# A third row tile loaded plainly and transposed on the array, so that three tiles' keys share the first weight chunks of a two-branch linear-attention kernel

## The chip, the core and the metric

The kernel runs on one core of a Trainium2 chip. The metric is the device time of one execution in microseconds, the median of several runs. The engines are called as the profile calls them: PE (matrix multiply), PEld (its weight loads), DVE (vector), ACT (activation), POOL, and SP, which only issues transfers. "SPq" and "ACTq" are the transfer queues of SP and ACT.

## What is computed

Two branches A and B have the same shape and the same input `x` (2048 rows of 640, bf16). Cut to what matters:

```python
def branch(x, wqkv, wo):                        # wqkv: 640 x 1920, 32 heads of 20
    q, k, v = split(x @ wqkv)
    phi = lambda t: where(t > 0, t + 1, exp(t)) + 1e-6
    pq, pk = phi(q), phi(k)
    kv, z = pk^T v, sum over rows of pk          # per head
    o = (pq @ kv) / (pq . z + 1e-6)
    return o @ wo

g = sigmoid((x * gate_w).sum(-1))
out = g * branch(x, A_wqkv, A_wo) + (1 - g) * branch(x, B_wqkv, B_wo)
```

## The kernel before

All work is cut into row tiles of 128 rows of `x` (16 tiles, `t` = 0 to 15) and contraction chunks of 128 of the 640 columns (5 chunks, `c` = 0 to 4).

The first stage computes the keys of both branches. It needs `x` with its columns on the partitions, in the buffer `XT`, as the stationary operand, and the key columns of `wqkv` in `WKW`, as the moving operand. One key step (`k_step(X, t, c, ps)`, lines 535 and 536) multiplies chunk c of tile t by chunk c of the weights of branch X: a matmul of 512 columns and one of 128 (129 for B, whose extra column is the gate). Five steps make one tile of one branch, accumulated in a pair of PSUM banks; the whole stage is 16 x 2 x 5 = 160 steps. After a tile, `k_post` makes phi of it: an exponential on ACT (L568) and two operations on DVE (L571, L579), after which the pair of banks is free.

How `XT` comes about differs by tile. Tiles 0 and 1 come by plain loads into `XN` (`ld_x`, tile 0 on SP's queue, tile 1 on ACT's) and are transposed on PE against an identity matrix (`x_tp`, L479), five transposes for each tile, which go into three PSUM banks; three copies (L496) take them to `XT`, on DVE for tile 0 and on ACT for tile 1. Tiles 2 to 15 come by transposing transfers from memory (`xt_dma`), and one later plain load (`xr`) brings their rows into `XN`, which the next stage reads.

SP issues the loads in the order written: x tile 0, the five 160 KB chunks of A's key weights, the five of B's, the seven transposing transfers, the rest. While the loads are issued, each is tied behind the one before on its queue (`o.behind`), so this order is the program's.

PE's order is the order of the calls: a planner picks, for the other engines, whichever of their operations can start first by its own costs, but for PE always the next one written. Its start is written out by hand. Warm-up matmuls (L466) come first, then the transposes of tiles 0 and 1, then A's keys of both tiles chunk by chunk (c outside, t inside), so that each landing chunk serves two tiles; `gate_col` (a small matmul, L516, and a DVE copy, L519, which put the gate vector beside B's weights) stands after the second chunk. Then come B's keys of tiles 0 and 1, also chunk by chunk, and then `k_unit(X, t)` for the other tiles, A and B in turn, each with its five steps in one go.

The later stages (the products of keys and `x`, line 643; queries, line 797; the small weights, 705 and 740; outputs, 957) follow on PE in the order written.

Of the kernel before, what the change touches and what calls it, by code (L numbers as in the profile page):

```python
# [6 lines left out]
ACT = mybir.ActivationFunctionType  # L7
# [3 lines left out]
S = 2048  # L11
D = 640
H = 32
NT = 16
NB = 4
NC = 5
# [60 lines left out]
class Sched:  # L77
# [7 lines left out]
    def op(self, eng, fn, cost, ins=(), outs=(), after=(), prio=None, name="", dma=None):  # L85
        if eng == "ACT" and dma is None:
            after = list(after) + self.consts
        o = Op(eng, fn, cost, list(ins), list(outs), after, len(self.ops) if prio is None else prio, name, dma)
        self.ops.append(o)
        return o  # L90
# [174 lines left out]
def body(nc, A_x, A_wqkv, A_wo, B_x, B_wqkv, B_wo, gate_w, out, log=None):  # L265
    no_start_barrier(nc)
    x = A_x[0]
# [8 lines left out]
    XN = sb("XN", [128, NT, XS_W], bf)  # L276
# [66 lines left out]
    def psw(b, w):  # L343
        return PS[:, b.slot : b.slot + b.n, :].rearrange("p a b -> p (a b)")[:, 0:w]
# [3 lines left out]
    def dma(q, name, dst, src, nbytes, ins=(), outs=(), after=(), issue=450.0, transpose=False, prio=None):  # L348
        timing = (330.0, 1500.0) if not transpose else (140.0, 1500.0) if loading else (1000.0, 1150.0)

        def fn(e):
            d = dst() if callable(dst) else dst
            with nc.allow_non_contiguous_dma(reason="layout"):
                return e.dma_start(d, src() if callable(src) else src, transpose=transpose)  # L354

        o = op(q, fn, 0.0, ins, outs, after, prio=prio, name=name, dma=(issue, nbytes) + timing)
        if loading:
            o.behind = chain.get(q)
            chain[q] = o
        return o  # L360

    def mm_cost(n):
        return n / 2.4 + 2.5

    def act_cost(n):
        return 190 + 0.833 * n

    def dve1(n):
        return 155 + 1.04 * n

    def dve4(n):
        return 150 + 0.27 * n


    bxn = [Buf("xn%d" % t) for t in range(NT)]
# [18 lines left out]
        outs=[bid],  # L394
# [9 lines left out]
    def ld_x(q, t):  # L404
        dma(q, "x%d" % t, XN[:, t, 0:D], x[128 * t : 128 * t + 128, :], 163840, outs=[bxn[t]])

    def ld_wk(q, X, c, after=()):
        dma(q, "wk%s%d" % (X, c), WK[X][:, c, 0:D], wqkv[X][128 * c : 128 * c + 128, D : 2 * D], 163840, outs=[bwk[X, c]], after=after)

    def xt_dma(t0, t1):  # L410
        dma(
            "SP",
            "xt%d" % t0,
            XT[:, :, 128 * t0 : 128 * t1],
            x[128 * t0 : 128 * t1, :],
            (t1 - t0) * 163840,
            outs=bxt[t0:t1],
            issue=(t1 - t0) * 1250.0,
            transpose=True,
        )  # L420
# [7 lines left out]
    for c in range(NC):  # L428
        if c == 0:
            ld_x("SP", c)  # L430
        ld_wk("SP", "A", c)
    for c in range(NC):
        ld_wk("SP", "B", c)
    for t0, t1 in ((2, 3), (3, 4), (4, 5), (5, 6), (6, 8), (8, 12), (12, 16)):
        xt_dma(t0, t1)
    dma("SP", "xr", XN[:, 2:NT, 0:D], x[256:S, :].rearrange("(t p) d -> p t d", p=128), 14 * 163840, outs=bxn[2:])
    for X in XS:
        dma("SP", "wq" + X, WQ[X][:, :, :], w3(X, 0), 819200, outs=[bwq[X]])
    for X in XS:
# [1 line left out]
    for X in XS:  # L441
        for r in range(2):
# [7 lines left out]
                outs=[bwo[X, r]],  # L450
# [11 lines left out]
    def warm(n, w=4):  # L462
        for i in range(n):
            op(
                "PE",
                lambda e: e.matmul(psw(bw, 128 * w), ONE[:, 0:1].to_broadcast([128, 128]), ONE[:, 0:1].to_broadcast([128, 128 * w]), start=True, stop=True),  # L466
                107.0 * w,
                ins=[bone],
                outs=[bw],
                name="warm",  # L470
            )

    def x_tp(t):
        for lo, hi in ((0, 1), (1, 3), (3, 5)):
            bt = Buf("tp", "ps")
            for c in range(lo, hi):
                op(
                    "PE",
                    lambda e, c=c, lo=lo, bt=bt: e.matmul(  # L479
                        PS[:, bt.slot, 128 * (c - lo) : 128 * (c - lo) + 128],  # L480
                        XN[:, t, 128 * c : 128 * c + 128],
                        IDN[:, :],
                        start=True,
                        stop=True,
                    ),
                    100.0,
                    ins=[bxn[t], bid],
                    outs=[bt],
                    name="tp%d" % t,
                )  # L490
            half = Buf("xth")

            def copy(e, lo=lo, hi=hi, bt=bt):
                o = XT[:, lo:hi, 128 * t : 128 * t + 128]
                i = PS[:, bt.slot, 0 : 128 * (hi - lo)].rearrange("p (c s) -> p c s", c=hi - lo)
                return e.activation(o, i, ACT.Copy) if t else e.tensor_copy(o, i)  # L496

            op(
                "ACT" if t else "DVE",
                copy,  # L500
                act_cost(128 * (hi - lo)) if t else dve1(128 * (hi - lo)),
                ins=[bt],
                outs=[half],
                name="tpc%d" % t,
            )
            bxt[t].parts = getattr(bxt[t], "parts", []) + [half] * (hi - lo)
# [22 lines left out]
    def k_step(X, t, c, ps):  # L529
        w = D + 1 if X == "B" else D  # L530

        def fn(e):
            a = psw(ps, w)
            l = XT[:, c, 128 * t : 128 * t + 128]
            e.matmul(a[:, 0:512], l, WK[X][:, c, 0:512], start=(c == 0), stop=(c == NC - 1))  # L535
            return e.matmul(a[:, 512:w], l, WK[X][:, c, 512:w], start=(c == 0), stop=(c == NC - 1))  # L536

        xin = [bxt[t].parts[c] if hasattr(bxt[t], "parts") else bxt[t]]
        op(
            "PE",  # L540
            fn,
            mm_cost(512) + mm_cost(128),
            ins=xin + [bwk[X, c]] + ([bgc] if X == "B" else []),
            outs=[ps],
            name="k%s%d_%d" % (X, t, c),
        )
# [3 lines left out]
    def k_post(X, t, ps):  # L550
        ek = Buf("ek", "ek")
        ek2 = Buf("ek2")
        pk = Buf("pk%s%d" % (X, t))
        bpk[X, t] = pk
        first = []
        if X == "B":
            b = Buf("ge")
            bge.append(b)
            op(
                "ACT",  # L560
                lambda e: e.activation(GE[:, t : t + 1], psw(ps, D + 1)[:, D : D + 1], ACT.Exp, scale=-1.0),
                200.0,
                ins=[ps],
                outs=[b],
                name="ge",
            )
            first = [b]
        op("ACT", lambda e: e.activation(EK[:, ek.slot, :], psw(ps, D), ACT.Exp), act_cost(D), ins=[ps] + first, outs=[ek], name="ke")  # L568
        op(
            "DVE",  # L570
            lambda e: e.tensor_scalar(EK[:, ek.slot, :], EK[:, ek.slot, :], 1.0, EPS, op0=ALU.min, op1=ALU.add),  # L571
            dve4(D),
            ins=[ek],
            outs=[ek2],
            name="kt",
        )
        op(
            "DVE",
            lambda e: e.scalar_tensor_tensor(PKt[X][:, t, :], psw(ps, D), 0.0, EK[:, ek.slot, :], op0=ALU.max, op1=ALU.add),  # L579
            dve1(D),  # L580
            ins=[ps, ek, ek2],
            outs=[pk],
            name="ks",
        )

    def k_unit(X, t):
        ps = Buf("k", "ps", 2)
        for c in range(NC):
            k_step(X, t, c, ps)
        k_post(X, t, ps)  # L590

    warm(4)
    warm(1, 2)
    pss = [Buf("k", "ps", 2) for _ in range(2)]
    x_tp(0)
    warm(1, 1)
    x_tp(1)
    for c in range(2):
        for t in range(2):
            k_step("A", t, c, pss[t])  # L600
    gate_col()
    for c in range(2, NC):
        for t in range(2):
            k_step("A", t, c, pss[t])
    for t in range(2):
        k_post("A", t, pss[t])
    pss = [Buf("k", "ps", 2) for _ in range(2)]
    for c in range(NC):
        for t in range(2):
            k_step("B", t, c, pss[t])  # L610
    for t in range(2):
        k_post("B", t, pss[t])
    for t in range(2, NT):
        for X in XS:
            k_unit(X, t)

# [10 lines left out]
        outs=[bgg2],  # L627
# [490 lines left out]
def bass_gated_mix__linear_attn_block__linear_attn_block__prompt_kernel(nc, *args):  # L1118
    body(nc, *args)
# [28 lines left out]
```

## Time and profile before

| | |
|---|---|
| time, median of 3 runs | 188.19 us (188.06 to 188.35) |
| span of the profiled execution | 186.3 us |
| PE busy | 183.4 us, 98% of the span |
| DVE, ACT busy | 136.9 us, 94.8 us |
| share of PE in the chain that ended last | 96% |

A busy time is the sum of an engine's instructions in the span. "The chain that ended last" is followed back from the last instruction: at each step to whatever released it. Since PE is nearly all of that chain, what changes the end is time that PE spends without an instruction, and instructions added to PE. Both lie, as far as this change is concerned, in the first microseconds, so the views that matter are PE's timeline there and the times in which the first loads land.

### The profile page before, as it was taken

How to read it: one execution, taken by the hardware profiler on the slowest of the kernel's cores; microseconds unless marked ns; L12 is line 12 of the kernel's file. 1: busy time of each engine (PE TensorE's matmuls, PEld its weight loads, DVE VectorE, ACT ScalarE, POOL GpSimd, SP SyncE). 2: the span in 40 equal slices, each digit the busy share in tenths (PEclk: the TensorE clock that was granted, in tenths of full speed). 3: DMA queues.
4: the chain of work that ended last, by engine and by line, in shares of the span. 5: the costliest groups of instructions: out<-in, count | busy, mean ns of one | idle time of the engine just before them, and what ended most of it. 6: DMA issues, size and time to landing. Idle time of an engine off the chain costs nothing.

```text
span 186.3 us, 3272 instructions
## 1 busy us (share of the span) xinstructions
PE 183.4 (98%) x1297; PEld 106.4 (57%) x1297; DVE 136.9 (73%) x264; ACT 94.8 (51%) x167; POOL 0.8 (0%) x10
## 2 busy tenths in 40 slices
PE   8999999999999999999999999999999999999995
PEld 4555555555555556555557555555567555555553
DVE  2389888888733546487699999998799996359563
ACT  4265656565554546544675666888523784400001
POOL 1000000000000000000000000000000000000000
PEclk9999999999999999999999999999999999999999
DMA  6979999995001011011611412125515347613434
GB/s 199 295 153 156 253 390 368 346 211 115 4 0 35 0 39 35 0 35 22 73 28 35 83 29 41 28 48 167 178 35 119 61 107 169 164 70 109 142 106 140
DMA packets 36501, 21.38 MB, mean 115 GB/s; under 512 B 25694, under 2 KB 36230, under 8 KB 36486
## 3 DMA queue, kind: packets, MB, share of 16 engines
q1 hardware_dynamic: 36188, 20.97, 44.0%
q8 instruction: 10, 0.16, 0.4%
q10 hardware_dynamic: 298, 0.20, 0.3%
q14 instruction: 5, 0.04, 0.1%
HBM read 10.87 MB, written 4.26 MB: 81 GB/s over the span
## 4 chain that ended last, share of the span: by engine, by line
PE 96%; DMA 2%; SPq 1%; DVE 0%; issue 0%; DVEq 0%
PE ps L957 23%; PE ps L797 23%; PE ps L643 19%; PE ps L535 18%; PE ps L644 5%; PE ps L536 5%; DMA WKW<-in_A_wqkv_dram 2%; PE ps L705 2%; PE ps L740 1%; SPq L354 1%; DVE TSB L1001 0%; DVEq L237 0%
## 5 line engine op out<-in xcount | busy, mean ns | idle before, releaser
L535 PE MATMUL ps<-WKW,XT 128*128 128x512 bf16 x160 | 44.0, 379 | 0.3 <-DMA WKW<-in_A_wqkv_dram 0.2
L814 ACT ACTIVATE EK<-ps 128x512 bf16<-128x512 f32 x40 | 23.9, 598 | 30.7 <-PE ps L797 30.7
L536 PE MATMUL ps<-WKW,XT 128*128 128x128 bf16 (+1 forms) x160 | 35.1, 219 | 0.0
L568 ACT ACTIVATE EK<-ps 128x640 bf16<-128x640 f32 x32 | 22.3, 704 | 9.9 <-DVE EK L571 5.0
L535 PEld LDWEIGHTS ps<-WKW,XT 128*128 128x128 bf16 x160 | 15.6, 98 | 19.4 <-DMA WKW<-in_A_wqkv_dram 0.7
L797 PE MATMUL ps<-XT,WQA 128*128 128x512 bf16 x100 | 24.5, 379 | 0.0
L797 PE MATMUL ps<-XT,WQB 128*128 128x512 bf16 x100 | 23.8, 380 | 0.0
L643 PE MATMUL ps<-XN,PKA 128*128 128x512 bf16 x80 | 23.5, 379 | 0.0
L643 PE MATMUL ps<-XN,PKB 128*128 128x512 bf16 x80 | 23.5, 379 | 0.0
L824 DVE TENSOR_SCALAR EK<-EK 128x512 bf16<-128x512 bf16 x40 | 11.6, 289 | 13.7 <-ACT EK L814 13.7
L644 PE MATMUL ps<-XN,PKA 128*128 128x129 bf16 x80 | 17.6, 220 | 0.0
L644 PE MATMUL ps<-XN,PKB 128*128 128x129 bf16 x80 | 17.6, 220 | 0.0
L957 PE MATMUL ps<-WPA,EX 128*128 128x512 bf16 x120 | 17.0, 299 | 0.0
L957 PE MATMUL ps<-WPB,PKA 128*128 128x512 bf16 x120 | 16.5, 299 | 0.0
L797 PEld LDWEIGHTS ps<-XT,WQB 128*128 128x128 bf16 x100 | 10.9, 118 | 8.9 <-issue 0.4
L571 DVE TENSOR_SCALAR EK<-EK 128x640 bf16<-128x640 bf16 x32 | 10.4, 325 | 7.2 <-ACT EK L568 7.1
L536 PEld LDWEIGHTS ps<-WKW,XT 128*128 128x128 bf16 x160 | 15.7, 98 | 0.0
L797 PEld LDWEIGHTS ps<-XT,WQA 128*128 128x128 bf16 x100 | 10.7, 117 | 8.1
L643 PEld LDWEIGHTS ps<-XN,PKA 128*128 128x128 bf16 x80 | 9.4, 117 | 7.9
L643 PEld LDWEIGHTS ps<-XN,PKB 128*128 128x128 bf16 x80 | 9.4, 117 | 7.9
L579 DVE SCALAR_TENSOR_TENSOR PKA<-ps,EK 128x640 bf16<-128x640 f32 x16 | 13.2, 825 | 0.6
L579 DVE SCALAR_TENSOR_TENSOR PKB<-ps,EK 128x640 bf16<-128x640 f32 x16 | 13.2, 825 | 0.6
(77 smaller groups left out, 222.2 us busy)
## 6 DMA issues: line engine op xcount, KB each, us to landing
out_dram<-TSB SPq DMA_DIRECT2D x15, 160.0 KB, 1.8
XN<-in_A_x_dram SPq DMA_DIRECT2D x1, 2240.0 KB, 9.6
WKW<-in_A_wqkv_dram SPq DMA_DIRECT2D x5, 160.0 KB, 4.0
WKW<-in_B_wqkv_dram SPq DMA_DIRECT2D x5, 160.0 KB, 3.9
WQA<-in_A_wqkv_dram SPq DMA_DIRECT2D x1, 800.0 KB, 11.2
WQB<-in_B_wqkv_dram SPq DMA_DIRECT2D x1, 800.0 KB, 12.4
WVA<-in_A_wqkv_dram SPq DMA_DIRECT2D x1, 800.0 KB, 12.6
WVB<-in_B_wqkv_dram SPq DMA_DIRECT2D x1, 800.0 KB, 13.8
```

The lines of the kernel that those rows point to most:

```text
L535: e.matmul(a[:, 0:512], l, WK[X][:, c, 0:512], start=(c == 0), stop=(c == NC - 1))
L536: return e.matmul(a[:, 512:w], l, WK[X][:, c, 512:w], start=(c == 0), stop=(c == NC - 1))
L568: op("ACT", lambda e: e.activation(EK[:, ek.slot, :], psw(ps, D), ACT.Exp), act_cost(D), ins=[ps] + first, outs=[ek], name="ke")
L571: lambda e: e.tensor_scalar(EK[:, ek.slot, :], EK[:, ek.slot, :], 1.0, EPS, op0=ALU.min, op1=ALU.add),
L579: lambda e: e.scalar_tensor_tensor(PKt[X][:, t, :], psw(ps, D), 0.0, EK[:, ek.slot, :], op0=ALU.max, op1=ALU.add),
L643: e.matmul(a[:, 0:512], l, XN[:, t, 0:512], start=(t == 0), stop=(t == NT - 1))
L644: return e.matmul(a[:, 512 : D + 1], l, XN[:, t, 512 : D + 1], start=(t == 0), stop=(t == NT - 1))
L705: r = e.matmul(PS[0:n, ps.slot, GR * i : GR * i + NC * w], WV[X][:, c, lo : lo + n], gv[:, c, :, 24 * u : 24 * u + w], start=(c == 0), sto ...
L797: r = e.matmul(PS[:, ps.slot, :], WQ[X][:, c, g::5], XT[:, c, 512 * b : 512 * b + 512], start=(c == 0), stop=(c == NC - 1),)
L814: lambda e: e.activation(EQ[:, eq.slot, :], PS[:, ps.slot, :], ACT.Exp),
L824: lambda e: e.tensor_scalar(EQ[:, eq.slot, :], EQ[:, eq.slot, :], 1.0, EPS, op0=ALU.min, op1=ALU.add),
L957: r = e.matmul(a[:, l0 - lo : h0 - lo], PQ[X, b][:, g, 128 * (t % 4) : 128 * (t % 4) + 128], WP[X][:, g, l0:h0], start=(X == first and g = ...
```

## The change

Tile 2 gets the treatment of tiles 0 and 1: a plain load on SP's queue right after the first weight chunk of A, five transposes on PE, and three copies, on DVE. The transposing transfers then begin with tile 3 and the later plain load with row 384. A's keys of three tiles are accumulated side by side, in three pairs of banks, so that each landing chunk can serve three tiles. Tile 2's transposes stand after the first chunk's steps of tiles 0 and 1, and its first two key steps after the second chunk's. B's keys are no longer taken chunk by chunk over two tiles; they follow as whole tiles 0, 1, 2, and from tile 3 on the order is the old one.

```diff
         if c == 0:
             ld_x("SP", c)
         ld_wk("SP", "A", c)
+        if c == 0:
+            ld_x("SP", 2)
     for c in range(NC):
         ld_wk("SP", "B", c)
-    for t0, t1 in ((2, 3), (3, 4), (4, 5), (5, 6), (6, 8), (8, 12), (12, 16)):
+    for t0, t1 in ((3, 4), (4, 5), (5, 6), (6, 8), (8, 12), (12, 16)):
         xt_dma(t0, t1)
-    dma("SP", "xr", XN[:, 2:NT, 0:D], x[256:S, :]...
+    dma("SP", "xr", XN[:, 3:NT, 0:D], x[384:S, :]...
...
-                return e.activation(o, i, ACT.Copy) if t else e.tensor_copy(o, i)
+                return e.activation(o, i, ACT.Copy) if t == 1 else e.tensor_copy(o, i)
...
-    pss = [Buf("k", "ps", 2) for _ in range(2)]
+    pss = [Buf("k", "ps", 2) for _ in range(3)]
     x_tp(0)
     warm(1, 1)
     x_tp(1)
+    for t in range(2):
+        k_step("A", t, 0, pss[t])
+    x_tp(2)
+    for t in range(2):
+        k_step("A", t, 1, pss[t])
     for c in range(2):
-        for t in range(2):
-            k_step("A", t, c, pss[t])
+        k_step("A", 2, c, pss[2])
     gate_col()
-    for c in range(2, NC):
+    for c in range(2, 4):
         for t in range(2):
             k_step("A", t, c, pss[t])
     for t in range(2):
+        k_step("A", t, 4, pss[t])
         k_post("A", t, pss[t])
-    pss = [Buf("k", "ps", 2) for _ in range(2)]
-    for c in range(NC):
-        for t in range(2):
-            k_step("B", t, c, pss[t])
-    for t in range(2):
-        k_post("B", t, pss[t])
-    for t in range(2, NT):
+    for c in range(2, NC):
+        k_step("A", 2, c, pss[2])
+    k_post("A", 2, pss[2])
+    for t in range(3):
+        k_unit("B", t)
+    for t in range(3, NT):
         for X in XS:
             k_unit(X, t)
```

More of the change, by code (lines that the diff above doesn't have):

```diff
@@ L431, in body @@
         ld_wk("SP", "A", c)
+        if c == 0:
+            ld_x("SP", 2)
     for c in range(NC):
         ld_wk("SP", "B", c)
-    for t0, t1 in ((2, 3), (3, 4), (4, 5), (5, 6), (6, 8), (8, 12), (12, 16)):
+    for t0, t1 in ((3, 4), (4, 5), (5, 6), (6, 8), (8, 12), (12, 16)):
         xt_dma(t0, t1)
-    dma("SP", "xr", XN[:, 2:NT, 0:D], x[256:S, :].rearrange("(t p) d -> p t d", p=128), 14 * 163840, outs=bxn[2:])
+    dma("SP", "xr", XN[:, 3:NT, 0:D], x[384:S, :].rearrange("(t p) d -> p t d", p=128), 13 * 163840, outs=bxn[3:])
     for X in XS:
@@ L495, in copy @@
                 i = PS[:, bt.slot, 0 : 128 * (hi - lo)].rearrange("p (c s) -> p c s", c=hi - lo)
-                return e.activation(o, i, ACT.Copy) if t else e.tensor_copy(o, i)
+                return e.activation(o, i, ACT.Copy) if t == 1 else e.tensor_copy(o, i)
             op(
-                "ACT" if t else "DVE",
+                "ACT" if t == 1 else "DVE",
                 copy,
-                act_cost(128 * (hi - lo)) if t else dve1(128 * (hi - lo)),
+                act_cost(128 * (hi - lo)) if t == 1 else dve1(128 * (hi - lo)),
                 ins=[bt],
```

## The prediction

> **What bounds the kernel now.** I read the page first, for the chain that ended last and the busy shares; then PE's timeline of the first 7 us; then the landing times of the first loads, one issue at a time; then the transfer rates in half-microsecond windows. From the page:
>
> ```profile
> PE 183.4 (98%) x1297; PEld 106.4 (57%) x1297; DVE 136.9 (73%) x264; ACT 94.8 (51%) x167; POOL 0.8 (0%) x10
> PE 96%; DMA 2%; SPq 1%; DVE 0%; issue 0%; DVEq 0%
> ```
>
> PE is the chain but for its beginning, where 2% (4.08 us from 1.38) is a load of A's weights. PE's timeline shows which one (start, length, line, operation):
>
> ```profile
> 3.25 0.58 PE L479 MATMUL ps<-IDN,XN 128*128 128x128 bf16 x5
> 3.67 0.38 PE L535 MATMUL ps<-WKW,XT 128*128 128x512 bf16 x1
> ...
> 4.07 0.38 PE L535 MATMUL ps<-WKW,XT 128*128 128x512 bf16 x1
> ...
> 4.63 0.39 PE L535 MATMUL ps<-WKW,XT 128*128 128x512 bf16 x1
> ...
> 4.91 0.38 PE L535 MATMUL ps<-WKW,XT 128*128 128x512 bf16 x1
> ...
> 5.18 0.17 PE L516 MATMUL ps<-IDN,GWZ 128*128 128x5 bf16 x1
> 5.51 0.39 PE L535 MATMUL ps<-WKW,XT 128*128 128x512 bf16 x1 [0.16 <-DMA WKW<-in_A_wqkv_dram]
> ...
> 5.79 0.38 PE L535 MATMUL ps<-WKW,XT 128*128 128x512 bf16 x1
> ...
> 6.06 0.38 PE L535 MATMUL ps<-WKW,XT 128*128 128x512 bf16 x1
> ```
>
> An unhindered key step follows the last one by 0.272 us (5.79 to 6.06). The first steps do not: 3.67, 4.07, 4.63, 4.91, 5.51. Steps for tile 0 and 1 of chunk 0 start at 3.67 and 4.07, of chunk 1 at 4.63 and 4.91, and chunk 2 begins at 5.51. These 1.84 us hold four steps (1.09) and the gate matmul (about 0.06), so PE waits 0.69 us: 0.13 for an ACT copy of tile 1, 0.29 for chunk 1, 0.27 for chunk 2. From 5.51 on I find no wider pitch than 0.272 to the end of the key stage: 156 steps in one run. So 0.69 us is all that a filler can save. What fixes 4.63 and 5.51 is the landing of chunks. Asked one issue at a time (last number: us from issue to landing), chunks 0, 1, 2 and 3 of A, issued at 0.45, 0.91, 1.38 and 1.84, give
>
> ```profile
> WKW<-in_A_wqkv_dram SPq DMA_DIRECT2D x1, 160.0 KB, 2.9
> ...
> WKW<-in_A_wqkv_dram SPq DMA_DIRECT2D x1, 160.0 KB, 3.7
> ...
> WKW<-in_A_wqkv_dram SPq DMA_DIRECT2D x1, 160.0 KB, 4.1
> ...
> WKW<-in_A_wqkv_dram SPq DMA_DIRECT2D x1, 160.0 KB, 4.0
> ```
>
> so they land at 3.35, 4.6, 5.5 and 5.85, and the next two, also near 4.0 after issues at 2.31 and 2.80, at 6.3 and 6.8. The last columns of two windows (granted clock, share of the transfer engines, GB/s) show why chunks 1 and 2 are late:
>
> ```profile
> 3.50:4.00 0.50, 0.50 (x7) 0.27 (x5) 0.43 (x2) 0.40 (x2) 0.00 (x0) 1.00 0.77 143
> 5.00:5.50 0.50, 0.35 (x5) 0.10 (x2) 0.11 (x1) 0.00 (x0) 0.00 (x0) 1.00 1.04 379
> ```
>
> Around 3.0 to 4.0 the rate falls to 190 and 143 GB/s although the engines are 77 to 84% occupied; afterwards it is 370 to 380, at which 160 KB take 0.43 us.
>
> **What the Trainium skill says.** "DMA: Bandwidth & Descriptors", section "Queues, rings and completion order": on each transfer engine descriptors are consumed in the order of the ring. A load put ahead of chunk 1 therefore delays chunk 1 to 4 and all of B. The trace agrees as far as it goes: landings come in the order of issue. The same page, "Why a DMA increments its semaphore by 16 and not by 1": a wait is over only when the slowest of the engines has finished. That fits a chunk held back while the mean rate is high, but the trace does not name the engine. The same page, "Issuing engines are not separate DMA queues": tile 1's load on ACT's queue uses the same engines; it landed after 2.8 us, SP's tile 0 after 2.5. "TensorE: Matmul & The Clock Gate", section "Wait — 56ns, not 53.3ns?", gives a warm start-to-start of 215.7 ns for 512 columns and 55.6 for 128, together 271; the trace has 272.
>
> **The change part by part.**
>
> *x tile 2 in the queue.* It takes the place of chunk 1 (issue at 0.91, 128 rows of 1280 bytes as before); chunk 1 takes that of chunk 2, and so on, one 0.46 us issue later each. If place in the queue decides, tile 2 lands at 4.6, chunk 1 at 5.5, chunk 2 at 5.85, chunk 3 at 6.3, chunk 4 at 6.8. Bounds for chunk 1: below, its old 4.6 plus the 0.43 us that 160 KB take, 5.03; above, another 0.4 beyond 5.5, one more trough. I take 5.5, since bytes ahead, sizes and issue times are then those of a measured case.
>
> *Tile 2's transposes on PE.* Tile 1's five started at 3.25 and the next step's weights load at 3.62: 0.37 us. They stand after the steps of chunk 0 (end 4.07 + 0.27 = 4.34) and run from 4.65 to 5.02. In this case they cost nothing themselves: PE would wait for chunk 1 anyway. But PE works in order: while it waits for tile 2, the chunk-1 steps of tiles 0 and 1, the gate matmul and everything else stand behind them.
>
> *The order after.* Let S be the start of the first chunk-1 step. Before, at 5.51, 4 steps and the gate were done and 156 remained. Now at S only 2 are done: 158 steps and the gate remain. If PE never waits again, the shift of the end is S - 5.51 + 2 x 0.272 + 0.06 = S - 4.91. With S = 5.52, 0.61 us later. This is the central sum.
>
> *Does PE wait again?* After S come 4 steps and the gate, 1.15 us, so chunk 2 is wanted at 6.67 (lands 5.85), chunk 3 at 7.2 (6.3), chunk 4 at 7.75 (6.8). Tile 2's steps need its copies: DVE, idle from 3.93, takes about 1.0 us for three (0.97 for tile 0's), 5.0 to 6.0, wanted in parts from 6.06. B begins after 13 A steps and the gate, at 9.1, when its chunks (6.8 to 8.5 before, 0.46 later now) are there, so taking B by whole tiles costs nothing. B's tile 1 needs the banks of A's tile 0: 18 steps and the gate after S, 4.96 us. That tile's last step ends 2.5 us after S, and before, its phi was finished 2.12 us after the step (6.88 to 9.00). That leaves some 0.3 us, so no wait, but the smallest margin here. The other edits lie off the path: six transposing transfers start 0.46 later but are one fewer, tile 3 is wanted only at about 13, and DVE and ACT do the same phi work, 1.15 us of DVE a tile against 1.36 of PE. From tile 3 on, the order of instructions is the old one, and PE, in one run, hands the shift to the end. Sum: 188.19 + 0.61 = 188.80 us.
>
> **The rivals.**
>
> *The trough belongs to A's rows, not to the time or the place* (for instance because chunks 1 and 2 read memory that answers slowly at first). Then x tile 2 passes quickly, by about 3.9, its transposes run at 4.34 to 4.71 in what was an idle gap, and chunk 1 lands at 4.6 + 0.43 = 5.03. S is 5.07, the shift 0.16: 188.35, within what can be told from no change. For it: chunk 0 landed only 2.9 after its issue, and the rate before 3.0 was already 322 to 395. Against: the low rate lasts a microsecond while two chunks and all engines are busy, and nothing ties it to rows.
>
> *The filler works and the queue has room*: tile 2 lands before 4.34 and chunk 1 by 4.71, almost where it did. Then S = 4.71 and the end is 0.20 earlier: 187.99, not slower. Against: 160 KB more must go through engines that are 77% or more occupied from 1.5 on. More than this cannot be won, as the transposes must follow 4.34.
>
> *A further wait.* Chunk 1 comes at 5.9, or the bank margin of 0.3 us is overdrawn, each some 0.4 more: 189.2. Against: the margins above; for: each of them rests on one trace.
>
> **How the numbers follow.** Place in the queue, 188.80: 50%. The trough bound to A's rows, 188.35: 31%. The filler without delay, 187.99: 6%. A further wait, 189.2: 8%. The remaining 5% are for something that the trace does not show and that gains more than 0.2% (0.38 us); by the sums above no mechanism of mine does. Slower by over 0.2% needs S above 5.29: the first and the fourth case, 0.58. Within 0.2%: the second and third, 0.37, of which I give 0.36. Faster: 0.06. The range reaches from the third case, with 0.1 for the runs' spread, to the further wait: 187.9 to 189.2.
>
> **What would show it.** In the profile after: the gap between the second chunk-0 step (4.07) and the first chunk-1 step, S. 5.5 shows the place in the queue, 5.1 the rows, 4.7 the filler. The second issue on SP's queue after the first weights lands near 4.6 or near 3.9. From S on, a pitch of 0.272 without gap to about 48.9, B's second tile included; a gap there before 12 us is the fourth case. I am wrong in kind if the total shift differs from S - 4.91, for then something after the key stage moved.

## The result, and the profile after

The changed kernel takes 189.75 us (189.49 to 190.39) against 188.12 us for the kernel before on the same chips: ratio 1.0094 [1.0070, 1.0118], 1.63 us slower by the medians. The prediction had 188.80. It named the sign and the first 0.6 us; about one microsecond more was lost late in the kernel, where the prediction had nothing.

From the page after:

```profile
PE 184.3 (98%) x1302; PEld 107.1 (57%) x1302; DVE 137.9 (73%) x267; ACT 95.1 (50%) x167; POOL 0.8 (0%) x10
...
PE 91%; DMA 5%; ACT 2%; issue 0%; DVE 0%; SPq 0%; DVEq 0%
```

PE has the five transposes more, DVE the three copies. New is the second line: PE's share of the chain that ended last fell from 96% to 91%, and 5% are transfers. PE's timeline after, at the place that the prediction named:

```profile
3.66 0.63 PE L537 MATMUL ps<-WKW,XT 128*128 128x512 bf16 x1
...
4.19 0.63 PE L537 MATMUL ps<-WKW,XT 128*128 128x512 bf16 x1
...
4.72 0.74 PE L481 MATMUL ps<-IDN,XN 128*128 128x128 bf16 x5
5.49 0.45 PE L537 MATMUL ps<-WKW,XT 128*128 128x512 bf16 x1
...
5.83 0.38 PE L537 MATMUL ps<-WKW,XT 128*128 128x512 bf16 x1
...
6.10 0.38 PE L537 MATMUL ps<-WKW,XT 128*128 128x512 bf16 x1
```

The first step of chunk 1 starts at S = 5.49; the forecast was 5.5. x tile 2 and A's chunk 1 are the third and fourth issue on SP's queue (last number: us from issue to landing):

```profile
XN<-in_A_x_dram SPq DMA_DIRECT2D x1, 160.0 KB, 3.7
...
WKW<-in_A_wqkv_dram SPq DMA_DIRECT2D x1, 160.0 KB, 4.1
```

They land 4.6 and 5.45 us into the span, as chunks 1 and 2 did before (forecast 4.6 and 5.5). Aligned instruction by instruction, PE then runs 0.61 us later than before, S - 4.91 + 0.03, through the key stage and on to 102 us. No gap follows S before 12 us; B's tile 1 did not wait for its banks.

What the prediction didn't have comes at the end. The chain that ended last, after (start, length, what):

```profile
153.21 5.03 DMA wpsB<-WKW
...
158.38 4.64 DMA WPB<-wpsB
...
163.15 22.19 PE ps L963 x165
...
185.43 0.29 DVE TSB L1007
```

B's small product matrix goes to memory in five stores (`wpsB`), and one load brings it back in another layout (`WPB`), which the outputs of B need. Before, the chain had one piece of PE from 150.17 to 184.25 there, since that load came in time. PE's timeline before, and then after, where the first of these outputs starts:

```profile
162.06 6.14 PE L957 MATMUL ps<-WPB,PKA 128*128 128x512 bf16 x44
```

```profile
163.15 5.05 PE L963 MATMUL ps<-WPB,PKA 128*128 128x512 bf16 x36 [0.52 <-DMA WPB<-wpsB]
```

PE waits here, and didn't before: the shift grows from 0.4 to 1.09 us (0.4, not 0.61, since the profile before loses some 0.2 us near 102 us, where PE's weight load waits for a DVE copy; the profile after does not). SP's issues show why the load is late; before, and then after:

```profile
151.26 2.78 SPq L354 DMA_DIRECT2D wpsB<-WKW  x5
...
156.54 0.35 SPq L354 DMA_DIRECT2D WPB<-wpsB  x1
```

```profile
151.67 2.77 SPq L354 DMA_DIRECT2D wpsB<-WKW  x5
...
158.38 0.35 SPq L354 DMA_DIRECT2D WPB<-wpsB  x1
```

The stores begin 0.41 us later, but the fourth, the last whose landing the trace gives, lands at 158.24 instead of 156.40, and the load follows. The second late loss is behind PE's end. SP's last wait, before and then after (total, times, longest):

```profile
SPq L1115 <- DMA out_dram<-TSB: 1.0, 2, 0.7
```

```profile
SPq L1121 <- DMA out_dram<-TSB: 1.9, 2, 1.7
```

The last output, of the same bytes, takes 1.0 us longer to land. So the profiled span is 2.1 us longer: 0.4 to 0.6 of it early, 0.5 to 0.7 at `WPB`, 1.0 at the last output. (These are one execution each; by the medians the difference is 1.63 us.)

### The profile page after: what moved, and what is told of

Read it like the earlier page. It is cut to its first block, busy times and chain, and to the rows that moved or that the text cites. A ratio compares the mean times of both kernels' runs of the same rounds, so it can differ in the third digit from the quotient of the medians.

```text
span 188.4 us, 3283 instructions
## 1 busy us (share of the span) xinstructions
PE 184.3 (98%) x1302; PEld 107.1 (57%) x1302; DVE 137.9 (73%) x267; ACT 95.1 (50%) x167; POOL 0.8 (0%) x10
## 4 chain that ended last, share of the span: by engine, by line
PE 91%; DMA 5%; ACT 2%; issue 0%; DVE 0%; SPq 0%; DVEq 0%
PE ps L803 23%; PE ps L537 19%; PE ps L649 18%; PE ps L963 17%; PE ps L538 5%; PE ps L650 5%; DMA wpsB<-WKW 3%; DMA WPB<-wpsB 2%; PE ps L711 2%; PE ps L468 1%; PE ps L481 1%; ACT WKW L761 1%; PE ps L746 1%; ACT PKB L987 1%; DVE TSB L1007 0%
## 5 line engine op out<-in xcount | busy, mean ns | idle before, releaser
L963 PEld LDWEIGHTS ps<-WPB,PKA 128*128 128x128 bf16 x120 | 9.2, 98 | 8.0 <-issue 1.0
```

Source lines behind the costliest of these rows:

```text
L963: r = e.matmul(a[:, l0 - lo : h0 - lo], PQ[X, b][:, g, 128 * (t % 4) : 128 * (t % 4) + 128], WP[X][:, g, l0:h0], start=(X == first and g = ...
```

## Where the later loss comes from: a theory

Both late transfers meet a kind of traffic that no line of the program issues. The page lists two queues of instructions beside queue 1, which carries SP's transfers, and queue 10, which carries ACT's (packets, MB, share of 16 transfer engines); before, and then after:

```profile
q8 instruction: 10, 0.16, 0.4%
...
q14 instruction: 5, 0.04, 0.1%
```

```profile
q8 instruction: 10, 0.16, 0.4%
...
q14 instruction: 6, 0.05, 0.1%
```

Queue 8 moves ten packets of 16 KB. In the trace they start every 256 or so records of PE (matmuls and weight loads): at records 178, 459, 698, ..., 2211, 2467 before, and at 218, 457, 708, ..., 2209, 2463 after. Queue 14 moves packets of 8 KB. Three of its six lie about 128 records of DVE apart, near 62, 190 and 318; the other three fit no such count and are left open here. The kernel before has 316 DVE records (the 264 of the page and the semaphore instructions): its last packet on queue 14 starts at 187.60, when the last output has landed. The changed kernel has 319: the packet starts at 186.66, during that output. PE has 10 records more (five transposes, five weight loads), so its ninth packet comes 10 records earlier in the program. Before it started at 156.26, after at 155.82, though PE runs later. Transfers in the 0.1 us in which each starts, after and then before:

```profile
q8 instruction: 1, 0.02, 95.4%
q1 hardware_dynamic: 54, 0.02, 73.4%
```

```profile
q8 instruction: 1, 0.02, 75.0%
q1 hardware_dynamic: 37, 0.01, 44.7%
```

In both the instructions share engines with the last stores of `wpsB` (queue 1), but after, more of the stores is still to come; the packet takes 1.53 us against 1.20. After it ends, at 157.35, one share of the stores goes on alone, one packet at a time, until they have landed at 158.24. Before, they had all been written by 156.54, well ahead of the packet's end at 157.46. The last output is alike. After, from 186.0 to 187.4 us, and then before, from 184.5 to 186.3:

```profile
q1 hardware_dynamic: 146, 0.13, 28.5%
q10 hardware_dynamic: 135, 0.03, 10.0%
q14 instruction: 1, 0.01, 2.5%
...
out_dram<-TSB ACTq DMA_DIRECT2D x1, 32.0 KB, 2.6
```

```profile
q1 hardware_dynamic: 268, 0.27, 44.0%
q10 hardware_dynamic: 144, 0.03, 8.3%
...
out_dram<-TSB ACTq DMA_DIRECT2D x1, 32.0 KB, 1.6
```

With the instruction packet in between, ACT's piece of the last output takes 2.6 us instead of 1.6 from issue to landing. The instruction packet runs from 186.66 to 187.23; fifteen of the output's 16 shares are written by 186.97, and the last one begins at 187.23, when the packet has ended, and is written at 187.83, 0.86 us after the others. The Trainium skill fits this: "Runtime: NRT & Kernel Launch", section "Instruction fetch mechanics", says that each engine's instructions stream through a queue of its own in blocks of 16 KiB, 256 instructions. PE's queue in this trace agrees (16 KB, some 256 records); what fits DVE, with 8 KB for some 128, differs in size, and queue 14 has three packets more. The page calls the cost of crossing a block "mostly hidden"; in the runs below, one such packet costs 0.85 us. "DMA: Bandwidth & Descriptors", section "Why a DMA increments its semaphore by 16 and not by 1", says that a wait is over when the slowest engine has finished, which is how one small packet on one transfer engine can hold a whole output: here 15 shares are done at 186.97, the last at 187.83.

The theory, called F in the texts below: the change adds a few instructions, the counts move two instruction packets into transfers that something waits for, and that makes up the loss beyond the queue's 0.6. Its rival, called T: the counts don't matter, and the late losses follow from the later start or the new order of work.

## The experiments

Each ratio is to the kernel before, measured beside the kernel in question: 187.96 us beside b_pe5, b_dve3, b_pe5_dve3 and a_act, 187.91 beside b_load, b_tiny, a_tiny and a_act_tiny, and 188.04 beside a_act2, a_act_fine, b_fine and a_late.

**Counts alone, in the kernel before.** `b_pe5` leaves everything as it is but the warm-up, whose matmuls it cuts finer. The expectation below counts five matmuls more; the kernel has six (12 records of PE), and 2560 columns instead of 2304.

```diff
...
-    warm(4)
+    warm(3)
+    warm(5, 1)
+    warm(2, 0.5)
     warm(1, 2)
```

> The kernel before, with its warm-up columns cut into five more matmuls (ten more PE instructions, nothing else moved). Theory F (instruction transfers): the 16 KB transfers on queue 8 are tied to PE's instruction count, so the one at 156.3 comes about 0.7 us earlier, beside the last stores of wpsB; these end near 158 instead of 156.4, the load of WPB lands about 1 us later, and PE waits about 0.7 us for it near 162: 188.8 us. Theory T (the late transfers are slow because the loads and the time were moved): nothing was moved, 188.1 us.

`b_dve3` adds three tiny DVE writes to an unused tile, at the very start:

```diff
+    PAD = sb("PAD", [128, 8], bf)
+    for i in range(3):
+        op("DVE", lambda e, i=i: e.memset(PAD[:, 2 * i : 2 * i + 2], 1.0), 60.0, prio=-1, name="pad")
```

> The kernel before, with three tiny DVE memsets at the very start, where DVE idles. Theory F: DVE's third 8 KB instruction transfer, which in the kernel before comes 1.3 us after the last output has landed, now comes while the last output is written, holds up one share of it by 1.0 us, and the time is 189.1 us; PE's last matmul does not move. Theory T: 188.1 us.

`b_pe5_dve3` has both edits.

> Both paddings in the kernel before. Theory F: the two holds add, 0.7 + 1.0, to 189.8 us, as slow as the changed kernel although no load, transpose or key step was touched. Theory T: 188.1 us.

| kernel | time, us | ratio to before |
|---|---|---|
| b_pe5 | 188.35 | 1.0015 [1.0004, 1.0026] |
| b_dve3 | 188.69 | 1.0045 [1.0027, 1.0062] |
| b_pe5_dve3 | 189.15 | 1.0072 [1.0050, 1.0093] |

Three writes of an unused tile, 180 us before the end, cost 0.85 us (0.0045 x 188). SP's last wait in the profile of b_dve3, and its queues from 184.6 to 187.3 us:

```profile
SPq L1118 <- DMA out_dram<-TSB: 2.2, 2, 2.0
```

```profile
q1 hardware_dynamic: 254, 0.25, 28.1%
q10 hardware_dynamic: 144, 0.03, 5.5%
q14 instruction: 1, 0.01, 0.7%
```

The longest wait is 2.0 us instead of 0.7, with the instruction packet beside it (185.94 to 186.25, and the late share begins at 186.25), while `WPB` was loaded as before (5.21 us after the first store) and PE's last matmul ended at 184.30 (184.24 before). This is the changed kernel's tail, made from the kernel before. In b_pe5 PE's ninth packet came at 154.75 instead of 156.26, and SP's issues read

```profile
150.81 2.76 SPq L354 DMA_DIRECT2D wpsB<-WKW  x5
...
156.77 0.35 SPq L354 DMA_DIRECT2D WPB<-wpsB  x1
```

5.96 us from the first store to the load, against 5.28 before. That is the sign expected, and the kernel is 0.28 us slower by the ratio, where 0.7 was expected. In this profile PE still did not wait for `WPB`: counted from the first store, it landed after 10.63 us instead of 10.25, and the time from its landing to its first use shrank from 0.55 to 0.17 us. This was the fastest of 22 executions; that others had no slack left is not shown. The 0.28 us are not lost at the start: with this edit the stage after the keys began at 47.72 and 47.74 us in two profiles, and at 47.97 and 48.17 in two without it. Both edits together give about the sum of the two (1.0060), and less than what was expected; in that profile PE ran some 0.2 us late at `WPB`.

**The count taken out of the changed kernel.** `a_act` gives tile 2's three copies to ACT, so that DVE has its old 316 records and PE its new 10. Nothing else differs.

```diff
-                return e.activation(o, i, ACT.Copy) if t == 1 else e.tensor_copy(o, i)
+                return e.activation(o, i, ACT.Copy) if t else e.tensor_copy(o, i)
...
-                "ACT" if t == 1 else "DVE",
+                "ACT" if t else "DVE",
```

> The changed kernel with the three copies of tile 2 on ACT instead of DVE. Theory F: DVE has the instruction count of the kernel before, its last instruction transfer falls after the end again, and about 1.0 us comes back: 188.75 us; the wait for WPB near 162 stays. Theory T: the copies are off the path either way, 189.75 us.

> The changed kernel with tile 2's copies on ACT once more, as the partner on the same chip of the two runs that follow: 0.9 us over the kernel before, 188.8 us.

It was measured twice, on two chips (as a_act and a_act2): 188.69 us, 1.0048 [1.0030, 1.0065], and 188.58 us, 1.0023 [1.0013, 1.0033]. Against 1.0094 for the changed kernel, which was not measured again beside them, 0.9 to 1.3 us came back. SP's last wait in a_act:

```profile
SPq L1121 <- DMA out_dram<-TSB: 1.0, 2, 0.8
```

The hold at the end is gone, as it is in every profile with 316 DVE records (nine kernels and a repeat, longest wait 0.7 to 0.8), and it is there in every one with 319 (four kernels, 1.5 to 2.0). The gap between the first store and the `WPB` load stayed long, 6.29 and 6.85 us, and PE was 0.15 us late at `WPB` in the one and waited 0.6 us in the other: that part is not DVE's.

**The place in the queue alone.** `b_load` loads x tile 2 behind A's first chunk, but uses neither the array transposes nor the new order; tile 2 still gets its transposing transfer too.

```diff
         ld_wk("SP", "A", c)
+        if c == 0:
+            ld_x("SP", 2)
...
-    dma("SP", "xr", XN[:, 2:NT, 0:D], x[256:S, :]...
+    dma("SP", "xr", XN[:, 3:NT, 0:D], x[384:S, :]...
```

> The kernel before, with only the plain load of x tile 2 put behind A's first chunk (tile 2 is still transposed by its own transfer, PE's and DVE's orders are untouched). If place in the queue decides: A's second chunk lands at 5.5 and the third at 5.85, the third chunk's steps begin at 6.1 instead of 5.5, 0.6 us late; 0.2 of it was absorbed near 102 in the changed kernel and will be here: 188.4 us. If the slow stretch belongs to A's rows: second chunk at 5.05, third at 5.9, 0.4 late, 0.2 at the end: 188.15 us.

188.19 us, 1.0019 [1.0005, 1.0034], so 0.36 us slower (0.1 to 0.6 by the interval, which holds both forecasts). PE's timeline:

```profile
5.12 0.39 PE L537 MATMUL ps<-WKW,XT 128*128 128x512 bf16 x1 [0.21 <-DMA WKW<-in_A_wqkv_dram]
...
5.40 0.38 PE L537 MATMUL ps<-WKW,XT 128*128 128x512 bf16 x1
...
5.70 0.38 PE L537 MATMUL ps<-WKW,XT 128*128 128x512 bf16 x1
```

Chunk 1 is used from 5.12 (4.63 before) and chunk 2 from 5.70 (5.51): here chunk 1 landed at 5.07, earlier than the 5.45 of the changed kernel's profile, and where the rival that blames A's rows puts it (5.05). What speaks against that rival is tile 2: it landed at 4.58 here, and at 4.61 to 4.84 in the six profiles of changed kernels that load it in this place, not at 3.9.

In the thirteen profiles other than a_late's, the third issue on SP's queue landed at 4.08 to 4.86 and the fourth at 5.04 to 5.67, over both orders of loads; so S in after, a_act, a_act2 and a_act_fine is 5.25 to 5.49, and one trace is not enough to place it. A more stable measure is the first matmul of the next stage: 47.59 to 48.17 us in five profiles with the old order (before, b_pe5, b_dve3, b_pe5_dve3, b_fine; mean 47.84), 48.28 to 48.58 in the four with the new (mean 48.42). The early loss is about 0.6 us.

**The order that the change wanted, with the load out of the way.** `a_late` is a_act with x tile 2 loaded behind A's chunk 2, its transposes after that chunk's steps, and its own five key steps after those of tiles 0 and 1.

```diff
-        if c == 0:
+        if c == 2:
             ld_x("SP", 2)
...
+    for t in range(2):
+        k_step("A", t, 2, pss[t])
+    x_tp(2)
...
-    for c in range(2, NC):
+    for c in range(NC):
         k_step("A", 2, c, pss[2])
```

> The changed kernel with the copies on ACT, but with x tile 2 loaded behind A's third chunk and transposed after that chunk's steps, so that no chunk that PE waits for is delayed. If the early loss is the place in the queue plus waiting for it, the loss changes from 0.5 us to the 0.37 us that the five transposes take in a busy stretch: 188.65 us. If the three-tile order itself could win, it would show here: below 188.0 us.

188.67 us, 1.0027 [1.0011, 1.0043]: no better than a_act2. PE's timeline:

```profile
5.95 0.39 PE L537 MATMUL ps<-WKW,XT 128*128 128x512 bf16 x1 [0.48 <-DMA WKW<-in_A_wqkv_dram]
...
6.50 0.44 PE L481 MATMUL ps<-IDN,XN 128*128 128x128 bf16 x5
6.78 0.38 PE L537 MATMUL ps<-WKW,XT 128*128 128x512 bf16 x1
```

The transposes now stand where PE is never short of work, and cost 0.28 us; the wait for chunk 2, before them, remains unfilled (it landed at 5.90, later than the fourth issue in any other profile). The next stage began at 48.69.

**Shifting PE's packet on purpose.** If 10 records bring the packet beside the stores, some 60 or 70 should bring it before them. `b_tiny` replaces part of the warm-up by 39 small matmuls (36 matmuls, so 72 records, more); `a_tiny` and `a_act_tiny` have the same edit in the changed kernel and in a_act.

```diff
-    warm(4)
-    warm(1, 2)
+    warm(2)
+    for i in range(39):
+        op("PE", ... matmul(psw(bw, 16)[0:32, :], ...)
```

> The kernel before with 36 more PE matmuls in the warm-up (72 instructions), tiny ones in place of most of the wide ones. Theory F: PE's ninth 16 KB instruction transfer moves from 156.3 to about 151, ahead of the stores of wpsB, and costs nothing, although ten instructions cost 0.4 us: 188.0 us. Theory that more PE instructions cost time in proportion: over 189 us.

> The changed kernel with the same 36 tiny matmuls. Theory F: the instruction transfer moves from 155.8 to about 151, the stores of wpsB end near 156.4 plus the 0.4 us by which all is late, PE waits no more for WPB, and 0.4 to 0.7 us come back: 189.2 us. The hold at the end stays. If the wait for WPB came from the later time itself: 189.75 us.

> The changed kernel with both remedies: tile 2's copies on ACT, and the 36 tiny matmuls. Theory F: only the late start is left, 0.4 us over the kernel before: 188.4 us. Otherwise nearer to 189.75 us.

Times and ratios: b_tiny 188.31, 1.0029 [1.0008, 1.0050]; a_tiny 189.06, 1.0053 [1.0033, 1.0074]; a_act_tiny 188.67, 1.0039 [1.0023, 1.0056]. For b_tiny this is a miss: after the small matmuls the array was still slow, the 512-column matmuls of its first key steps took 0.63 us instead of 0.38 until about 6 us, and in the three kernels the next stage began at 48.7 to 49.0. So these times don't measure the packet. The traces do: the packet came at 152.1 to 152.6, 0.3 to 0.5 us after the first store was issued, where it was expected ahead of the stores; the gap from the first store to the load was 5.45 to 5.62 us, and PE waited for `WPB` in none of the three. a_tiny, with 319 DVE records, kept the hold at the end (1.5 us).

`b_fine` and `a_act_fine` repeat it with a warm-up of 36 matmuls of 64 columns (31 matmuls, so 62 records, more), after which the key steps were at full pace by 4.3 us. ("That kernel" in the second text is a_act2.)

```diff
-    warm(4)
-    warm(1, 2)
+    for i in range(36):
+        op("PE", ... matmul(psw(bw, 64)[0:32, :], ...)
```

> The kernel before with the same 36 warm-up matmuls, the control for the warm-up itself: 188.0 us under both theories; anything above is the price of the finer warm-up.

> That kernel with its five wide warm-up matmuls cut into 36 of 64 columns (31 matmuls, 62 PE instructions more), which keep PE as busy over the same time as before. Theory F: the ninth instruction transfer of PE moves to before the stores of wpsB, these and the issue of the load of WPB take 5.3 to 5.6 us from first issue instead of 6.3, PE has no wait for WPB, and 0.3 us come back: 188.4 us. If only the early stage is slower: no change, 188.8 us.

b_fine: 187.93 us, 0.9991 [0.9977, 1.0006], so 62 records of PE cost nothing in themselves. a_act_fine: 188.39 us, 1.0023 [1.0009, 1.0036], against 188.58 and the same ratio for a_act2. SP's issues in a_act_fine:

```profile
151.85 3.61 SPq L354 DMA_DIRECT2D wpsB<-WKW  x5
...
157.48 0.35 SPq L354 DMA_DIRECT2D WPB<-wpsB  x1
```

The gap is 5.63 us, 1.2 us less than a_act2's 6.85, and no wait for `WPB` is left in its profile. But the five stores now take SP 3.61 us to issue instead of 2.77, as in the three kernels before it, PE has a new wait of 0.3 us at 142.45 for another load (`GSB`), and the gain, 0.19 us by the medians, is not resolved. None of these kernels beats the one before.

## Why the prediction was wrong

*Place in the queue* (first part of the working): right for tile 2 and for the order. Tile 2 and chunks 1 to 4 landed at 4.64, 5.45, 5.84, 6.26 and 6.83, against 4.6, 5.5, 5.85, 6.3 and 6.8; b_load alone costs 0.36 us. That chunk 1 fits so well is in part luck: in the six other profiles with tile 2 in this place it landed at 5.04 to 5.22, near the lower bound of the working (5.03). The rival that ties the slow stretch to A's rows would have had tile 2 by 3.9; with 4.58 to 4.84 in seven profiles it falls. (One reading of the working is too smooth: from 4.0 to 4.5 us the rate before was 284 GB/s, and 370 to 380 only from 4.5 on.)

*S - 4.91*: right to 0.03 us for this profile, though S varies by 0.24 from profile to profile and the forecast took one trace's values as fixed. The five transposes hid beside the wait for chunk 1, as costed, in this profile and in a_act's. They need not: the array can still run at half pace there (in the profile after, chunk 0's steps follow each other by 0.53 us, not 0.27), and then they take 0.53 us instead of 0.37. In a_act2 they started at 4.96 and S was 5.49, although chunk 1 had landed at 5.22; PE had no wait there, so the transposes set S.

*No wait in the key stage*: right; the gap-free run from S on is there.

*"From tile 3 on, the order of instructions is the old one, and PE, in one run, hands the shift to the end."* This is the step that failed. The order is the old one, and yet PE did not stay in one run, because the load of `WPB` lost its slack (0.5 us of waiting); and behind PE's last matmul the landing of the last output grew by 1.0 us. The prediction's own sign of being wrong in kind, a total shift other than S - 4.91, came true: 1.63 us against 0.58. None of its cases had a loss after the key stage.

*"The other edits lie off the path"*: the term that was costed at nothing. I priced ten PE records and three DVE copies by their duration and what hides it. What they cost, by the runs, is that with them the later instruction packets of their engine come earlier in the program. Measured in the kernel before, without any of the change: 0.85 us for three DVE instructions (b_dve3), 0.28 for twelve of PE (b_pe5), where the change has ten. With the early 0.36 to 0.6 that makes 1.5 to 1.7 us, against 1.63 by the medians and 1.77 by the ratio; the terms' intervals are wide enough that this agreement proves little by itself.

How far each is shown: DVE's part by adding the count (b_dve3), by taking it away (a_act), and by the hold that is in every trace with 319 records and in none with 316. For PE's part the traces show the mechanism, and the times show the price less well. In all six profiles with these 10 or 12 records more, the packet comes at 154.7 to 156.1 us, the last share of the stores lands 0.7 to 0.9 us after the packet has ended, and the gap from the first store to the load is 5.96 to 6.85 us. In the three with the old count the packet comes at 156.3 to 156.7, the stores have landed about 1 us before it ends, and the gap is 5.21 to 5.34. With the packet at 152.1 to 152.6 the gap is 5.45 to 5.64. But the packets do not keep strictly to the count: in b_fine the ninth came some 28 records later than in the kernel before, at 153.33, and the gap is 5.98, without a wait and without a loss of time (its start was quicker, the next stage at 47.59). The wait that follows a long gap was 0 to 0.7 us from profile to profile, and the time that a_act_fine wins is not resolved. So the price of PE's part, about 0.3 us, stays uncertain. That a packet of queue 14 near these records is DVE's was inferred from the counts, which b_dve3 and a_act bear out; the trace does not name the engine that fetches.

## What to carry to other kernels

Count the instructions that an edit adds to each engine, not only their time: find in the trace where the instruction packets fall, and see whether the new count pushes one into a transfer that something waits for, above all the last output or a store that is read back. A filler for a wait must bring its own operand without delaying what is waited for; here the filler's load took the place in the queue of the very chunk that PE waited for. And add to the chain of waits the slack of the next transfer behind it: the 0.55 us at `WPB` was less than what the change cost there.

## What was not expected of the hardware

- One instruction packet of 8 KB beside the last output kept one of its 16 shares waiting until the packet had ended: written 0.6 to 1.1 us after the other 15 in four profiles, of an output that takes 1.6 us in all from issue to landing. Three DVE instructions at the start of the kernel decided it (188.69 against 187.96 us).
- A 16 KB instruction packet took 1.0 to 1.5 us beside the stores, and the last share of the stores landed 0.7 to 0.9 us after its end: in the changed kernel at 158.24 instead of 156.40, of which 0.41 us are the later start.
- The same kernel on two chips came out at 1.0048 [1.0030, 1.0065] and 1.0023 [1.0013, 1.0033], intervals that barely touch. An interval covers the runs beside each other, so a difference of 0.2% between kernels measured apart should not be read here; its cause is open.
